# Moving the second half's weight loads behind the stores of x, tile 4's scores into slab 0, and the second pass's loads ahead in slab 8

## The chip, the cores and the metric

The kernel runs on one core of a Trainium2 chip. The metric is the device time of one execution in microseconds. Before the change it is 1320.05 us, the median of three runs (1319.97 to 1320.37). Names: TensorE (PE in the profile, PEld its weight loads), VectorE (DVE), ScalarE (ACT), GpSimd (POOL), SyncE (SP, which here issues every DMA).

## The reference, cut to what matters

Three layers follow each other on 4608 rows (8 batches of 576) of 512 columns:

```
scores = (q_c @ k_c^T) / 8            # chunks of 64 rows, 8 heads
attn = softmax(scores);  x = attn @ v # rows of 8 heads x 64 = 512 columns
xn = (x - mean) / sqrt(var + 1e-6) * g_ln
x2 = x + relu(xn @ w_ch1) @ w_ch2     # 512 -> 2048 -> 512
h = relu(x2 @ w_in)                   # 512 -> 1024
h = h * sigmoid(conv3(h, conv_w))     # three taps along the rows
out = h @ w_out                       # 1024 -> 512
```

The weights come as 64-bit numbers. Each matrix product is made of three matmuls on a high and a low part.

## The kernel before, in words

The rows are 36 tiles of 128, grouped in nine slabs of four tiles (512 rows). There are three passes.

**First pass.** For each tile `Attention` has one-letter steps: L loads q, k and v; S makes scores on TensorE; M takes their maxima on DVE; E is eight exponentials on ACT; R is a reciprocal on DVE; P transposes on TensorE; C copies on ACT; V multiplies by v on TensorE; X scales on DVE and stores x to DRAM (`xd`); B, x, T and e normalise the tile and put it, transposed, into the slab's block. `product` (L580) then multiplies the slab by w_ch1. It uses a scheme of seven products on quartered matrices, n = 1 to 7, for each of four column groups G. A slab so has 28 slots (`SLOTS`, L627). Its results are stored to `hd`.

w_ch1 is prepared from 64-bit numbers by `Block`, in sixteen pieces: W loads piece i, a is an ACT instruction (L134), t, m and n are DVE instructions (L140, L146, L152), g scales on ACT, s are sums on DVE, h and l make the high part (ACT) and the low part (DVE). W0 to W7 are the first half, which groups G = 0 and 1 need, W8 to W15 the second half, for G = 2 and 3. In the profile W is `w<-in_moe_w_ch_dram`.

The order is written out by hand. The string `START` (L18) lists the steps ahead of slab 0 and, behind the bar, those that are put into slab 0's slots one group after the other, separated by slashes. An engine works through its own instructions in this order, and so does SP with the DMAs. `session` (L634) places a tile's V, S of the next tile and so on into slots; L668 says at which slot the sessions of tiles 4 to 7 begin. Tiles use two buffers for q and k, three for v and two for x (tags `rq`, `rk`, `rv`, `x`), so that L4 waits for S2 and V1, L5 for S3 and V2, and X2 for the store of X0.

**Second pass.** `Down` (L670) loads a piece of `hd` (tag `hr`, three buffers of 512 KB), splits it into `hh` (ACT) and `hl` (DVE) and multiplies by w_ch2 (`w2`): 9 slabs of 16 steps. w_ch2 is prepared by `Piece`s: `cv_load` loads one, `cv_step` (L220) does one step of a pipeline of four (h, a, m, l) over the pieces. All this is begun in slab 8, behind the pool `dp` that takes the place of the attention's buffers from slot (G, s) = (0, 5). Four pieces lie in `dp` (`wd0` to `wd3`). The other twelve take the room of w_ch1's first half, from slot (2, 5) on. At a slab's end `finish` (L756) adds the residual and puts four `store`s into a list; each transposes a quarter on DVE into `x2T` and stores it to `x2d`. They are taken off one at a time in the next slab. Those of the last slab come together ahead of the third pass (L832).

**Third pass.** `Gate` and `outtile`: w_in, the taps, the gate, w_out. Gates write TensorE's banks 4 to 7 in turn, and `outtile` (L851) reads the high and low parts `Gh` and `Gl` of all eight gates.

Of the kernel before, what the change touches and what calls it, by code (L numbers as in the profile page):

```python
# [8 lines left out]
F32 = mybir.dt.float32  # L9
# [6 lines left out]


START = """  # L18
W0 W2 L0 W1 W3 L1 W4 W6 W5 L2 W7 L3 W8 W10 L4 W9 W11 W12 W14 W13 W15 L5
a0 t0 m0 n0 a2 t2 g0 m2 h0 n2 l0 g2 S0 M0 a1 t1 E0 m1 n1 t3 a3 P0 R0 g1  # L20
m3 C0 n3 S1 h1 g3 l1 V0 M1 h2 a4 l2 E1 X0 s0 t4 s2 a6 P1 s1 a5 t5 h4 s3
C1 m5 h3 l4 V1 m4 S2 l3 t6 h5 R1 m6 a7 t7 M2 X1 E2 n5 S3 B1 B0 g5 P2 R2
C2 M3 V2 y0 E3 n6 z0 y1 m7 n4 g6 P3 R3 n7 e0 X2 C3 z1 g7 l5 V3 e1 B2 h9
S4 X3 u1 h8 s4 g4 M4 h6 s6 h7 s5 E4 l6 s7 B3 h11 P4 y2 C4 l11 z2 y3 e2 l7
z3 v1 e3 l9 l8 u3 j0 u2 h10 v3 u5 v2 l10 v5 h12 j1 l12 u7 j2 h13 v7 u6 j3 l13
u4 v6 v4 R4
|
a8 t8 a10 t10 m8 n8
/ g8 a9 t9 m10 n10
/ g10 a11 a12 t11 t12 m9  # L30
/ a14 n9 t14 g9 m12
/ h14 n12 m11 g12 n11 a13
/ l14 t13 g11 m14 h15
/ n14 s8 g14 l15 a15
# [11 lines left out]
def attn_moe_moe2(  # L46
# [34 lines left out]
    NF1 = w_ch1.shape[1] // 128  # L81
# [174 lines left out]
    def add_w2(f, pool, tag):  # L256
        add(rows(w_ch2, f), w2, f, pool, tag)
# [261 lines left out]
    with tc.manual_schedule():  # L519
# [145 lines left out]
        for tv in range(4, NTILE):  # L665

            t = 28 * (tv // 4 - 1) + 7 * (tv % 4 - 1) + 1
            session({4: 1, 5: 8, 6: 12, 7: 16}.get(tv, t), tv)  # L668

        class Down:  # L670

# [21 lines left out]
            def down(self, f, hh, hl):  # L693
                for i in range(4):
                    s = slice(i * 128, (i + 1) * 128)
                    mm3(self.acc[i], hh[:, s], hl[:, s], w2[f][:, 0, :], w2[f][:, 1, :],
                        f == 0, f == NF1 - 1)

        F_ORDER = [f + 8 * i for f in range(8) for i in range(2)]
        dp = None  # L700
        for p in range(NS + 1):
            if p + 1 < NS:
                slabs[p + 1] = Slab(p + 1)
            for G in range(4):
                for s, (n, lag) in enumerate(SLOTS):
                    t = 28 * p + 7 * G + s
                    pp, GG = (p, G - lag) if G >= lag else (p - 1, 3)
                    if 0 <= pp < NS:
                        product(pp, GG, n)
                        nxt = slabs.get(pp + 1)  # L710
                        if GG == 3 and nxt:
                            if n == 1:
                                nxt.j(0)
                                nxt.j(1)
                            nxt.both(n)
                    for fn in events.pop(t, ()):
# [24 lines left out]
        su_p.release()
# [49 lines left out]
        downs = {0: down}  # L791
        xrs = {}
        for n, (p, f) in enumerate(todo):
            if n == 0:
                parts = down.split(f)
            hh, hl = parts

            if f < 8:
                ahead = p * 8 + f + 2
                if ahead < 8 * NS:  # L800
                    if ahead % 8 == 0:
                        downs[ahead // 8] = Down(ahead // 8)
# [12 lines left out]
            if (p, f) == (0, 15):  # L815
# [4 lines left out]
                for i in range(16):  # L820
                    pool, tag = wb_tags[i]
# [191 lines left out]
```

## Time and profile before

| what | value |
|---|---|
| median of three runs | 1320.05 us |
| the profiled execution, its own time | 1322.7 us |
| its span | 1320.8 us |
| TensorE busy | 1247.7 us (94%) |
| VectorE busy | 749.0 us (57%) |
| ScalarE busy | 615.6 us (47%) |
| mean granted TensorE clock | 0.968 |
| chain that ended last | TensorE 88%, DMA 5%, DVE 4%, ACT 2% |

The span runs from the first to the last instruction of the profiled execution; 1.9 us of its own time lie around it. The first pass begins its first product at 62.24 us, the second pass begins at 521.76 us and the third at 919.82 us of the span. In a timeline's row the bracket at the end is the idle time of the engine before this instruction and what released it.

### The profile page before, as it was taken

The page shows a single profiled execution, that of the slowest core. Times are in us where ns is not written, and L with a number is a line of the kernel's source. Part 1 is how long each engine was busy: PE and PEld are TensorE (multiplying, and loading weights), DVE is VectorE, ACT ScalarE, POOL GpSimd, SP SyncE. Part 2 cuts the span into 40 slices and gives each one's busy share as a digit, 9 for nine tenths or more (in the row PEclk, how much of TensorE's full clock was granted, in tenths as well). Part 3 has the DMA queues.
Part 4 walks back from the last instruction along what each step waited for, and adds up shares of the span by engine and source line. Part 5 has one row for each costly group of instructions (what it writes and reads, how often), then busy time and mean ns, then how long its engine had stood idle before and what let it go on. Part 6 is the DMA issues. An engine that isn't in the chain of part 4 may idle for free.

```text
span 1320.8 us, 23297 instructions
## 1 busy us (share of the span) xinstructions
PE 1247.7 (94%) x9096; PEld 1088.2 (82%) x9096; DVE 749.0 (57%) x1430; ACT 615.6 (47%) x1510; POOL 75.1 (6%) x172
## 2 busy tenths in 40 slices
PE   5468999999999996999999999999999999999998
PEld 4367999999999995787888888888888888888887
DVE  6597565565566455757743333433886555655550
ACT  6575565555565443433422223222675555555541
POOL 0000000000000000000000000000121111111000
PEclk6588999999999998999999999999999999999999
DMA  9523555545554348376543456443111011101001
GB/s 259 171 87 123 192 184 176 178 172 190 185 186 166 131 160 326 120 236 231 196 159 120 149 178 196 132 135 112 48 57 56 25 56 57 56 25 56 25 24 48
DMA packets 127021, 177.70 MB, mean 135 GB/s; under 512 B 12736, under 2 KB 72128, under 8 KB 126912
## 3 DMA queue, kind: packets, MB, share of 16 engines
q1 hardware_dynamic: 126912, 176.22, 40.2%
q8 instruction: 71, 1.16, 0.4%
q14 instruction: 38, 0.31, 0.1%
HBM read 110.13 MB, written 66.06 MB: 133 GB/s over the span
## 4 chain that ended last, share of the span: by engine, by line
PE 88%; DMA 5%; DVE 4%; ACT 2%; SPq 0%; issue 0%; POOL 0%; DVEq 0%; ACTq 0%; POOLq 0%
PE banks L114 28%; PE banks L115 27%; PE banks L116 27%; DMA w<-in_moe_w_ch_dram 2%; PE banks L381 2%; PE banks L463 1%; DMA rq<-in_q_dram 1%; PE banks L421 1%; DVE w L157 1%; DMA hr<-hd 1%; DMA xd<-x 1%; DMA wd<-in_moe_w_ch_dram 0%; DVE xr L160 0%; ACT pp L407 0%; ACT w L336 0%
## 5 line engine op out<-in xcount | busy, mean ns | idle before, releaser
L114 PE MATMUL banks<-xc,w 128*128 128x256 f32 x1008 | 289.9, 288 | 6.6 <-ACT u L606 5.8
L115 PE MATMUL banks<-xc,w 128*128 128x256 f32 x1008 | 282.6, 280 | 0.6 <-DVE xc L157 0.6
L116 PE MATMUL banks<-xc,w 128*128 128x256 f32 x1008 | 282.1, 280 | 0.0
L686 ACT ACTIVATE hh<-hr 128x512 fp32r<-128x512 f32 x144 | 90.9, 632 | 279.0 <-PE banks L116 269.5
L687 DVE SCALAR_TENSOR_TENSOR hl<-hr,hh 128x512 fp32r<-128x512 f32 x144 | 99.2, 690 | 204.9 <-ACT hh L686 204.9
L114 PEld LDWEIGHTS banks<-xc,w 128*128 128x128 f32 x1008 | 192.5, 191 | 10.0 <-ACT u L606 6.5
L115 PEld LDWEIGHTS banks<-xc,w 128*128 128x128 f32 x1008 | 192.9, 191 | 0.8 <-DVE xc L157 0.8
L116 PEld LDWEIGHTS banks<-xc,w 128*128 128x128 f32 x1008 | 192.7, 191 | 0.0
L114 PE MATMUL banks<-w,hl 128*128 128x512 f32 x432 | 168.5, 390 | 0.0
L115 PE MATMUL banks<-w,hh 128*128 128x512 f32 x432 | 168.1, 389 | 0.0
L116 PE MATMUL banks<-w,hh 128*128 128x512 f32 x432 | 168.1, 389 | 0.0
L897 DVE SCALAR_TENSOR_TENSOR cv<-hb,cw_sb,cv 128x510 f32<-128x510 f32 (+31 forms) x256 | 117.3, 513 | 0.6
L115 PE MATMUL banks<-xb,w 128*128 128x512 f32 x288 | 113.0, 392 | 0.0
L114 PE MATMUL banks<-xb,w 128*128 128x512 f32 x288 | 112.9, 392 | 0.0
L116 PE MATMUL banks<-xb,w 128*128 128x512 f32 x288 | 112.8, 392 | 0.0
L160 DVE TENSOR_TENSOR u<-banks,u 128x512 f32<-128x512 f32 x108 | 73.6, 689 | 60.0 <-ACT u L606 32.8
L114 PEld LDWEIGHTS banks<-w,hl 128*128 128x128 f32 x432 | 81.1, 188 | 18.3 <-DVE hl L687 1.4
L116 PEld LDWEIGHTS banks<-w,hh 128*128 128x128 f32 x432 | 81.1, 188 | 17.0
L115 PEld LDWEIGHTS banks<-w,hh 128*128 128x128 f32 x432 | 81.1, 188 | 16.5
L606 ACT COPY u<-banks 128x512 f32<-128x512 f32 x108 | 64.0, 593 | 59.9 <-PE banks L116 56.8
L407 ACT ACTIVATE pp<-banks,mx 128x64 f32<-128x64 f32 x288 | 87.7, 333 | 3.3 <-DVE mx L398 2.8
L115 PE MATMUL banks<-w,Gh 128*128 128x512 f32 x216 | 84.3, 390 | 0.0
(106 smaller groups left out, 2095.0 us busy)
## 6 DMA issues: line engine op xcount, KB each, us to landing
hd<-u SPq DMA_DIRECT2D x144, 256.0 KB, 3.0
hr<-hd SPq DMA_DIRECT2D x72, 512.0 KB, 4.1
w<-in_moe_w_ch_dram SPq DMA_DIRECT2D x28, 512.0 KB, 7.6
rv<-in_v_dram SPq DMA_DIRECT2D x36, 256.0 KB, 4.0
xd<-x SPq DMA_DIRECT2D x36, 256.0 KB, 2.0
xr<-xd SPq DMA_DIRECT2D x36, 256.0 KB, 5.1
x2d<-x2T SPq DMA_DIRECT2D x36, 256.0 KB, 2.1
x2r<-x2d SPq DMA_DIRECT2D x36, 256.0 KB, 4.1
```

The lines of the kernel that those rows point to most:

```text
L114: nc.tensor.matmul(ps, ll, rh, start=first, stop=False, **kw)
L115: nc.tensor.matmul(ps, lh, rl, start=False, stop=False, **kw)
L116: nc.tensor.matmul(ps, lh, rh, start=False, stop=last, **kw)
L157: nc.vector.tensor_tensor(out=out, in0=a, in1=b, op=ALU.subtract)
L160: nc.vector.tensor_tensor(out=out, in0=a, in1=b, op=ALU.add)
L381: nc.tensor.matmul(ps[half(c), e, j, :], lt[half(e), j, c, :], rt[half(e), j, c, :], start=True, stop=True,)
L407: nc.scalar.activation(out=pp[:, j, e, :], in_=self.both[T][:, e, j, :], func=AF.Exp, scale=SCALE, bias=mx[:, e, j:j + 1], accum_out=sm[:, ...
L421: nc.tensor.transpose(tp[:, j * 128:(j + 1) * 128], pp[:, j].rearrange("p e k -> p (e k)"), ident)
L606: nc.scalar.copy(flat(t), bank[to])
L686: nc.scalar.activation(out=self.hh, in_=t, func=AF.Relu)
L687: nc.vector.scalar_tensor_tensor(out=self.hl, in0=t, scalar=0.0, in1=self.hh.bitcast(F32), op0=ALU.max, op1=ALU.subtract,)
L897: nc.vector.scalar_tensor_tensor(out=cv[:, a:e], in0=hb[:, a + tap:e + tap], scalar=cw_sb[:, tap, f:f + 1], in1=cv[:, a:e], op0=ALU.mult, ...
```

## The change

`START` loses W8 to W15, L4 and L5 from its first lines; they stand behind the stores that belong to X1, X2 and X3. W7 goes ahead of L2. S4, M4 and E4 go from the part ahead of slab 0 into its slot 0, R4 and P4 into slot 2, C4 into slot 3. The other steps ahead of slab 0 are put into another order. The sessions of tiles 4 to 7 begin one slot later, that of tile 4 four slots later.

In slab 8, the second pass's first three loads of `hd` are issued at slot (0, 5), ahead of the loads of w_ch2. Five pieces of w_ch2 instead of four lie in `dp`. The steps of `cv_step` are left out of slots (2, 6) to (3, 6) but for (3, 1), (3, 3) and (3, 5). The first split is made at slot (3, 4). Later loads of `hd` are issued at odd steps for three pieces ahead, instead of at even steps for two. `x2T` has one buffer instead of two.

```diff
 START = """
-W0 W2 L0 W1 W3 L1 W4 W6 W5 L2 W7 L3 W8 W10 L4 W9 W11 W12 W14 W13 W15 L5
-a0 t0 m0 n0 a2 t2 g0 m2 h0 n2 l0 g2 S0 M0 a1 t1 E0 m1 n1 t3 a3 P0 R0 g1
...
-S4 X3 u1 h8 s4 g4 M4 h6 s6 h7 s5 E4 l6 s7 B3 h11 P4 y2 C4 l11 z2 y3 e2 l7
...
+W0 W2 L0 W1 W3 L1 W4 W6 W5 W7 L2 L3 a0 t0 m0 n0 a2 t2 g0 m2 h0 n2 l0 g2
...
+E1 X0 s0 t6 s2 a6 s1 P1 a5 t5 s3 h4 R1 h3 m6 C1 l2 m5 V1 B0 S2 X1 W8 W10
...
+R3 g7 y0 l5 C3 z0 y1 h9 V3 X2 W9 W11 L4 W12 e0 l9 g4 z1 X3 W14 W13 W15 L5 h8
...
 |
-a8 t8 a10 t10 m8 n8
+S4 M4 E4 a8 t8 a10 t10 m8 n8
 / g8 a9 t9 m10 n10
-/ g10 a11 a12 t11 t12 m9
-/ a14 n9 t14 g9 m12
+/ g10 a11 a12 t11 t12 m9 R4 P4
+/ C4 a14 n9 t14 g9 m12
...
-            session({4: 1, 5: 8, 6: 12, 7: 16}.get(tv, t), tv)
+            session({4: 5, 5: 9, 6: 13, 7: 17}.get(tv, t), tv)
...
+        EARLY = 5
...
-                            for i, f in enumerate(F_ORDER[:4]):
+                            down = Down(0)
+                            for f in range(3):
+                                down.load(f)
+                            for i, f in enumerate(F_ORDER[:EARLY]):
                                 add_w2(f, lambda: dp, f"wd{i}")
                             cv_load(2)
...
-                            cv_load(12)
-                        elif (G, s) > (0, 5) and s % 2 == 0:
+                            cv_load(NF1)
+                        elif (0, 5) < (G, s) < (2, 5) and s % 2 == 0 or (G, s) in ((3, 1), (3, 3), (3, 5)):
                             cv_step()
-                        if (G, s) == (3, 2):
-                            down = Down(0)
-                            for f in range(2):
-                                down.load(f)
+                        if (G, s) == (3, 4):
+                            parts = down.split(0)
...
-                    x2T = dp.tile([128, 512], F32, tag="x2T", bufs=2, name="x2T")
+                    x2T = dp.tile([128, 512], F32, tag="x2T", bufs=1, name="x2T")
...
-            if n == 0:
-                parts = down.split(f)
...
-            if f < 8:
-                ahead = p * 8 + f + 2
+            if f >= 8:
+                ahead = p * 8 + f % 8 + 3
```

On SP's queue, ahead of slab 0, before the change (the last of the second half's weights, then L5, then the first stores of x, `xd_99` being that of tile 0):

```order
L125 DMA w_281<-in_moe_w_ch_dram 128x1024
L125 DMA w_283<-in_moe_w_ch_dram 128x1024
L125 DMA w_285<-in_moe_w_ch_dram 128x1024
L366 DMA rq<-in_q_dram 64x2x256 x2
L366 DMA rk<-in_k_dram 64x2x256 x2
L375 DMA rv<-in_v_dram 128x512
L439 DMA xd_99<-x 128x512
L439 DMA xd_100<-x 128x512
L439 DMA xd_101<-x 128x512
```

The same place now, from L3 on:

```order
L365 DMA rq<-in_q_dram 64x2x256 x2
L365 DMA rk<-in_k_dram 64x2x256 x2
L374 DMA rv<-in_v_dram 128x512
L438 DMA xd_99<-x 128x512
L438 DMA xd_100<-x 128x512
L124 DMA w_449<-in_moe_w_ch_dram 128x1024
L124 DMA w_451<-in_moe_w_ch_dram 128x1024
L438 DMA xd_101<-x 128x512
L124 DMA w_579<-in_moe_w_ch_dram 128x1024
L124 DMA w_581<-in_moe_w_ch_dram 128x1024
```

The first stores have gone from behind L5 to right behind L3, with W8 and W10 (`w_449`, `w_451`) next.

On ACT, at slab 0's slot 0, before (`u_749` is the copy of its first product, L134 the steps a8 and a10, L311 g8):

```order
L606 COPY u_749<-banks 128x512
L134 ACTIVATE w_751<-w_263 128x512
L134 ACTIVATE w_754<-w_265 128x512
L311 ACTIVATE w_751<-w_751,g_sb 128x512
L134 ACTIVATE w_751<-w_275 128x512
```

and now:

```order
L605 COPY u_712<-banks 128x512
L406 ACTIVATE pp,sm<-banks,mx 128x64 x8
L133 ACTIVATE w_743<-w_449 128x512
L133 ACTIVATE w_746<-w_451 128x512
L310 ACTIVATE w_743<-w_743,g_sb 128x512
```

E4's eight exponentials now stand ahead of a8.

On SP's queue in slab 8, around slot (0, 5), before (`hd_0_167` is a store of the slab's own results, `wd` a piece of w_ch2):

```order
L601 DMA hd_0_167<-u_6583 128x512
L125 DMA wd_6664<-in_moe_w_ch_dram 128x1024
L125 DMA wd_6666<-in_moe_w_ch_dram 128x1024
L601 DMA hd_0_167<-u_6680 128x512
L125 DMA wd_6686<-in_moe_w_ch_dram 128x1024
```

and now:

```order
L600 DMA hd_0_167<-u_6583 128x512
L679 DMA hr<-hd_0_135 128x4x256 x2
L679 DMA hr<-hd_1_136 128x4x256
L124 DMA wd_6670<-in_moe_w_ch_dram 128x1024
L124 DMA wd_6672<-in_moe_w_ch_dram 128x1024
L600 DMA hd_0_167<-u_6686 128x512
```

Three loads of 512 KB for the second pass stand ahead of the first weight piece.

## Rows read from the trace of the kernel before

**Rows 1.** The page's 40 slices of the span, TensorE's busy share in tenths.

```profile
PE   5468999999999996999999999999999999999998
```

**Rows 2.** Stretches: busy us (instructions) per engine, granted clock, DMA share, GB/s.

```profile
0.00:30.00 30.00, 15.97 (x192) 12.19 (x192) 18.83 (x38) 17.91 (x54) 0.85 (x8) 0.67 0.97 253
...
60.00:90.00 30.00, 20.57 (x239) 19.07 (x238) 29.25 (x58) 21.86 (x50) 0.63 (x2) 0.80 0.18 54
```

**Rows 3.** The chain that ended last: start us, us, what.

```profile
44.31 6.91 DMA xd<-x
...
96.80 1.20 ACT pp L407 x8
...
510.01 10.32 DMA hr<-hd
```

**Rows 4.** DVE's timeline ahead of and in slab 0.

```profile
29.50 0.43 DVE L140 TENSOR_SCALAR w<-w 128x512 int32<-128x512 uint32 x1 [1.97 <-DMA w<-in_moe_w_ch_dram]
...
51.32 0.69 DVE L435 TENSOR_TENSOR x<-banks,sm 128x512 f32<-128x512 f32 x1 [12.72 <-DMA xd<-x]
...
71.45 0.71 DVE L140 TENSOR_SCALAR w<-w 128x512 int32<-128x512 uint32 x2
...
73.41 0.68 DVE L397 TENSOR_REDUCE mx<-banks 128x8 f32<-128x512 f32 x1
...
109.29 0.69 DVE L445 BATCH_NORM_STATS2 bs<-x 128x6 f32<-128x512 f32 x1
...
110.30 0.68 DVE L157 TENSOR_TENSOR w<-w,w 128x512 fp32r<-128x512 f32 x1
...
113.09 0.69 DVE L157 TENSOR_TENSOR w<-s,w 128x512 fp32r<-128x512 f32 x1 [0.68 <-ACT w L336]
```

**Rows 5.** ACT's timeline in slab 0: a8 and a10, then a15.

```profile
70.44 1.23 ACT L134 ACTIVATE w<-w 128x512 f32<-128x512 f32 x2
...
87.53 0.68 ACT L134 ACTIVATE w<-w 128x512 f32<-128x512 f32 x1
```

**Rows 6.** TensorE's timeline in slab 8 and into the second pass.

```profile
480.56 0.39 PE L114 MATMUL banks<-xc,w 128*128 128x256 f32 x1 [1.95 <-ACT u L606]
...
503.17 0.39 PE L114 MATMUL banks<-xc,w 128*128 128x256 f32 x1 [1.65 <-ACT u L606]
...
509.57 0.38 PE L114 MATMUL banks<-xc,w 128*128 128x256 f32 x1 [0.68 <-ACT u L606]
...
521.76 0.29 PEld L114 LDWEIGHTS banks<-wd,hl 128*128 128x128 f32 x1 [9.38 <-DVE hl L687]
```

**Rows 7.** ACT's timeline in slab 8: the first two pieces of w_ch2.

```profile
479.34 0.69 ACT L134 ACTIVATE cy<-wd 128x512 f32<-128x512 f32 x1 [4.18 <-DMA wd<-in_moe_w_ch_dram]
...
480.99 0.67 ACT L134 ACTIVATE cy<-wd 128x512 f32<-128x512 f32 x1 [0.48 <-DMA wd<-in_moe_w_ch_dram]
```

**Rows 8.** Stretches of slab 8 and the second pass's start.

```profile
478.40:487.00 8.60, 6.65 (x44) 6.46 (x44) 5.21 (x9) 5.07 (x9) 0.00 (x0) 0.80 0.66 249
487.00:498.00 11.00, 11.00 (x100) 11.00 (x99) 7.45 (x13) 3.98 (x7) 0.00 (x0) 1.00 0.35 126
...
521.70:527.00 5.30, 5.24 (x15) 4.18 (x16) 2.94 (x6) 1.27 (x3) 0.00 (x0) 0.62 1.00 346
527.00:537.00 10.00, 10.00 (x46) 8.26 (x45) 9.49 (x17) 6.68 (x12) 0.00 (x0) 1.00 0.20 64
```

**Rows 9.** DVE's timeline at the third pass's start, and the low part of gate 7.

```profile
920.63 1.29 DVE L762 STREAM_TRANSPOSE x2T<-xr 128x512 f32<-128x512 f32 x2
923.47 1.37 DVE L762 STREAM_TRANSPOSE x2T<-xr 128x512 f32<-128x512 f32 x2 [1.55 <-DMA x2d<-x2T]
...
956.00 0.69 DVE L931 TENSOR_TENSOR Gl<-gt,Gh 128x511 fp32r<-128x511 f32 x1
```

**Rows 10.** ACT's timeline at the third pass's start.

```profile
927.07 0.72 ACT L886 ACTIVATE cv<-hb,cw_sb 128x511 f32<-128x511 f32 x1 [0.85 <-DMA x2d<-x2T]
```

**Rows 11.** TensorE's timeline: the first `outtile` reads gate 7's low part.

```profile
957.90 0.39 PE L114 MATMUL banks<-wx,Gl 128*128 128x512 f32 x1
```

More of the change, by code (lines that the diff above doesn't have):

```diff
@@ L18 @@
 START = """
-W0 W2 L0 W1 W3 L1 W4 W6 W5 L2 W7 L3 W8 W10 L4 W9 W11 W12 W14 W13 W15 L5
-a0 t0 m0 n0 a2 t2 g0 m2 h0 n2 l0 g2 S0 M0 a1 t1 E0 m1 n1 t3 a3 P0 R0 g1
-m3 C0 n3 S1 h1 g3 l1 V0 M1 h2 a4 l2 E1 X0 s0 t4 s2 a6 P1 s1 a5 t5 h4 s3
-C1 m5 h3 l4 V1 m4 S2 l3 t6 h5 R1 m6 a7 t7 M2 X1 E2 n5 S3 B1 B0 g5 P2 R2
-C2 M3 V2 y0 E3 n6 z0 y1 m7 n4 g6 P3 R3 n7 e0 X2 C3 z1 g7 l5 V3 e1 B2 h9
-S4 X3 u1 h8 s4 g4 M4 h6 s6 h7 s5 E4 l6 s7 B3 h11 P4 y2 C4 l11 z2 y3 e2 l7
-z3 v1 e3 l9 l8 u3 j0 u2 h10 v3 u5 v2 l10 v5 h12 j1 l12 u7 j2 h13 v7 u6 j3 l13
-u4 v6 v4 R4
+W0 W2 L0 W1 W3 L1 W4 W6 W5 W7 L2 L3 a0 t0 m0 n0 a2 t2 g0 m2 h0 n2 l0 g2
+S0 M0 a1 t1 E0 m1 n1 t3 a3 P0 R0 g1 m3 C0 n3 S1 h1 g3 l1 V0 M1 h2 a4 t4
+E1 X0 s0 t6 s2 a6 s1 P1 a5 t5 s3 h4 R1 h3 m6 C1 l2 m5 V1 B0 S2 X1 W8 W10
+a7 t7 M2 m7 E2 n5 l3 S3 n6 m4 g5 P2 M3 g6 C2 n4 E3 V2 l4 n7 B1 h5 R2 P3
+R3 g7 y0 l5 C3 z0 y1 h9 V3 X2 W9 W11 L4 W12 e0 l9 g4 z1 X3 W14 W13 W15 L5 h8
+h7 B2 e1 B3 h6 u1 l7 v1 y3 l8 z3 s4 e3 y2 s6 z2 s5 e2 l6 h11 j0 u2 j1 u3
+s7 u5 v3 u7 h10 l11 j2 l10 u6 v2 h12 v6 j3 l12 u4 v5 h13 v4 l13 v7
 |
-a8 t8 a10 t10 m8 n8
+S4 M4 E4 a8 t8 a10 t10 m8 n8
 / g8 a9 t9 m10 n10
-/ g10 a11 a12 t11 t12 m9
-/ a14 n9 t14 g9 m12
+/ g10 a11 a12 t11 t12 m9 R4 P4
+/ C4 a14 n9 t14 g9 m12
 / h14 n12 m11 g12 n11 a13
@@ L729, in attn_moe_moe2 @@
                             tags = [f"w0{kk}{i}" for kk in range(2) for i in range(7)]
-                            for f, tag in zip(F_ORDER[4:], tags):
+                            for f, tag in zip(F_ORDER[EARLY:], tags):
                                 add_w2(f, lambda: wa_p, tag)
-                            cv_load(12)
-                        elif (G, s) > (0, 5) and s % 2 == 0:
+                            cv_load(NF1)
+                        elif (0, 5) < (G, s) < (2, 5) and s % 2 == 0 or (G, s) in ((3, 1), (3, 3), (3, 5)):
                             cv_step()
-                        if (G, s) == (3, 2):
-                            down = Down(0)
-                            for f in range(2):
-                                down.load(f)
+                        if (G, s) == (3, 4):
+                            parts = down.split(0)
         su_p.release()
```

## The prediction, made before the changed kernel was run

> **What bounds the kernel now.** I read the page's slices first. TensorE is busy all along except in two places: the first slices, ahead of and in slab 0, and the slices around 480 to 520 us [rows 1]. What the change saves must come out of these two, so I went on with stretches, then with the chain of waits, then with each engine's timeline there.
>
> Ahead of slab 0 and in its first half the engine that sets the pace is DVE, which prepares w_ch1: in 60 to 90 us it is busy for 29.25 of 30 us, TensorE for 20.57 [rows 2]. The one long hole in DVE's time is the instruction X2, which waits 12.72 us, to 51.32, for the store of X0 [rows 4]. The chain says why: that store is issued only at 44.31 and takes 6.91 us to land [rows 3], for in SP's order it stands behind all sixteen weight pieces and L5. TensorE runs on without holes when the list of weight steps ends, with DVE's last low part at 113.09 [rows 4].
>
> Around 480 to 520 us slab 8 goes over into the second pass. TensorE's timeline has four holes there: 1.95, 1.65 and 0.68 us for ACT's copies out of its banks, and 9.38 us for the first `hl` [rows 6]. The copies are late because ACT stands in front of a weight piece that hasn't landed (4.18 us for the first) [rows 7], the `hl` because its load of `hd`, issued at 510.01 behind twelve weight loads, lands after 10.32 us [rows 3].
>
> The sum below is made against the profiled execution (1322.7 us, span 1320.8). It lies 2.65 us above the median of 1320.05; I take the same saving off the median.
>
> **Term 1, ahead of and in slab 0.** The store of X0 now stands right behind L3 and is long landed when X2 comes: **-12.7 us** on DVE. W7 ahead of L2 takes away DVE's wait of 1.97 us for W7 [rows 4], and L2's transfers, S2 and M2 come later by about one weight load (1.65 us, from the two landings seen at 479.34 and 480.99 [rows 7]); I let the two cancel. M4, some 0.7 us (the maximum at 73.41 [rows 4]), only moves along DVE's queue. E4 does cost something: it was hidden in ACT's idle time during the 12.72 us, and now stands ahead of a8 in slot 0, with DVE's m8 behind a8. M4 must first get through on DVE, then ACT needs 2 x 1.20 us for eight exponentials [rows 3] and about 0.6 for a8 [rows 5], of which DVE fills 0.71 with t8 and t10 [rows 4]: 2.4 + 0.6 - 0.7 = **+2.3 us**. The session of tile 6 begins at slot 13 instead of 12, so that its statistics (109.29 to 110.30 [rows 4]) come behind the list's last weight step: **-1.0 us**. Sum: -12.7 + 2.3 - 1.0 = **-11.4 us**. The weight loads themselves I cost at nothing: W8 follows X1's store, some 30 us ahead of a8, and the first 30 us move 253 GB/s [rows 2], so that eight loads of 0.52 MB take some 17 us; if this cover goes, each late load stops ACT and DVE in turn (a rival below). Bounds: 7 us saved (ACT behind the exponentials and copies also stops DVE later in slab 0, about twice the 2.3) to 15 us (DVE's small waits for ACT near 113 us go too).
>
> **Term 2, slab 8.** Removed: with `hd` loaded at slot (0, 5) and split at (3, 4), the hole of 9.38 us goes. With no weight step between (2, 5) and (3, 1), ACT's stop at 502 us goes, and with it 1.65 + 0.68 us. The half clock behind the 9.38 us goes too: in 521.7 to 527 us the granted clock is 0.62 (that is, partly 1.2 GHz) and 15 matmuls take 5.24 us, where 46 take 10.00 at full clock [rows 8]: 15 x (0.349 - 0.217) = 2.0 us. Removed in all: 9.4 + 1.65 + 0.7 + 2.0 = 13.7 us.
>
> Added: at (0, 5) three loads of 512 KB now stand ahead of the first weight piece, and the step at (0, 6) still makes ACT wait for that piece, with the copy behind it that frees TensorE's bank. No row shows these loads in this place. If the transfers overlapped fully, the piece would land as now: 0. If each took the 4.18 us that ACT waited for one [rows 7], end to end, 12.5 us. The nearest row is the spacing of two weight loads issued together, 480.99 - 479.34 = 1.65 us [rows 7], and the load of `hd` behind twelve others that took 10.32 us [rows 3] shows that later loads do wait their turn: 3 x 1.65 = **+5.0 us**. The hole of 1.95 us becomes 6.9. After it there is a stretch at half clock already now (clock 0.80; 44 matmuls in 6.65 us where 100 take 11.00 [rows 8]: 44 x (0.151 - 0.110) = 1.8 us); after a longer hole I take the 2.0 us seen behind the 9.38: +0.2. Term 2: -13.7 + 5.0 + 0.2 = **-8.5 us**, bounds -13.5 and -1.
>
> The Trainium skill, page "DMA: Bandwidth & Descriptors", section "Queues, rings and completion order", says that a DMA engine consumes the descriptors of one ring in order; by that rule the weight piece does wait for the three loads, which speaks against this order of issue, and the row of 10.32 us agrees. From the ceiling of 435 GB/s in the same page's "Specifications" the three loads would take 3.6 us, an estimate, and the result would be 1.4 us lower.
>
> Costed at nothing: the fifth piece in `dp` (its steps fill the eight slots up to (2, 4)); the later loads of `hd` (three steps ahead, queued behind nothing that waits); the weight steps moved out of slab 8 (the last piece is ready five steps ahead of its use, and DVE's work in each step of the second pass stays the same).
>
> **Term 3, the third pass's start.** With one `x2T`, the last slab's four transposes run one after the other with their stores. The row at 923.47 shows the interval: it waited for the store of the one at 920.63, 2.84 us [rows 9]. The fourth so begins at 920.63 + 3 x 2.84 = 929.15 instead of about 924.1: DVE 5.0 us late. What comes next on ACT had already waited 0.85 us for such a store [rows 10], and the chain of gates has 957.90 - 956.69 = 1.2 us to spare when TensorE needs gate 7's low part [rows 9, 11]; the banks of the gates leave about as much. Up to there ACT and DVE wait for each other and catch nothing up: 5.0 - 0.85 - 1.2 = **+3.0 us**. Bounds: 0 (four banks of lead hide it) and 5.0. Inside the second pass the stores come 5 us apart, more than 2.84, and cost nothing.
>
> **Sum**: -11.4 - 8.5 + 3.0 = -16.9 us; 1320.05 - 16.9 = 1303.15, rounded to **1303 us** (a profiled execution would stand near 1306).
>
> **The rivals.**
> A. *The loads of `hd` don't delay the weight piece*: SP issues them in time that the transfers don't need, and ACT waits its 4.18 us as now. For it: the DMA engines are not full at this place (share 0.66 in 478.4 to 487 [rows 8]). Against it: the 10.32 us. Then 5.2 us less: 1298 us.
> B. *The third pass hides its late start.* For it: TensorE does not wait once there now. Against it: 1.2 us to spare only. Then 1300 us.
> C. *Slab 0 keeps more*: with E4 and a tighter row of sessions ACT becomes the bound between slots 0 and 13. For it: E4 comes in addition to ACT's 21.86 us of 30 [rows 2]. Against it: 8 us of idle time are left there. Term 1 at -7: 1307.5 us.
> D. *The change doesn't take the wait away*: X2 or X3 waits as long for something else, such as V2. Against it: L2 and L3 still stand ahead of every store. Then term 1 is near 0: 1314.5 us.
> E. *Slower: the second half's weights come too late for slab 0.* Six of them, L4 and L5 are now issued only behind the stores of X2 and X3, at about 39 us (51.32 - 12.72 [rows 4]). If queued loads landed 10.32 us apart, as long as that one load took [rows 3], the sixth would land at 39 + 62 = 101; from its a step (a15, 87.53 [rows 5]) to the list's end DVE needs 113.8 - 87.5 = 26 us, so the list ends at 127 instead of 113.8: +13.5, less the 5.5 of terms 2 and 3, so 1328 us. It decides from (113.8 + 5.5 - 26 - 39) / 6 = 9 us a load. Against it: 253 GB/s, or 2 us a load [rows 2].
>
> **How the numbers follow.** Forecast 0.50, A 0.15, B 0.10, C 0.17, D 0.05, E 0.03. The range of **1296 to 1311** takes in A and B, alone or with term 1 at its upper bound in part (1303 - 5.2 - 3 = 1295), and on the other side C, or the loads of `hd` end to end (+7.5: 1310.5). What is left out is D, E and the joint ends. About 0.2% (2.6 us) is what a measurement of this kernel can tell from no change. Every case but E lies over 0.2% below 1320.05: faster 0.95; same 0.02, for several upper bounds together; slower 0.03.
>
> **What would show it.** In the changed profile: no wait of DVE for `xd<-x`; TensorE's unbroken work from about 104 us; DVE idle some 2 us behind M4 in slot 0; in slab 8 ACT waiting some 9 us for `wd` and TensorE with one hole of about 7 us, then half clock, but no hole ahead of the second pass; four single transposes 2.84 us apart at the end, and short waits of TensorE in the third pass's first ten gates. A hole of 2 us in slab 8 would prove term 2 wrong on `hd`; DVE or ACT waiting for `w<-in_moe_w_ch_dram` in slab 0 would prove rival E right.

## The result, and the profile after

The changed kernel takes **1309.25 us** (median of 4 runs, 1308.23 to 1310.14), the kernel before beside it 1320.21 (4 runs, 1319.97 to 1322.01): a ratio of 0.9914 with an interval of 0.9897 to 0.9931, so 9.1 to 13.6 us less, 11.3 by the ratio in the middle. The forecast was 1303, 16.9 us less. The profiled execution took 1309.48 us (span 1307.5).

Every stage can be dated by one row of TensorE's timeline. I use five marks throughout, and the end of the span (session 8 is that of tile 8, session 35 that of the last tile):

| mark (us from the span's start) | before | after | difference | gained in the stage |
|---|---|---|---|---|
| session 8's product with v | 127.91 | 118.00 | -9.91 | -9.91 |
| session 35's product with v | 447.19 | 437.21 | -9.98 | -0.07 |
| second pass, first matmul | 521.76 | 505.70 | -16.06 | -6.08 |
| third pass, first gate | 919.82 | 903.25 | -16.57 | -0.51 |
| third pass, first output tile | 953.12 | 939.81 | -13.31 | +3.26 |
| end of the span | 1320.8 | 1307.5 | -13.3 | 0 |

So the two profiles differ by 13.3 us where the ratio of the medians gives 11.3; the profiled execution of before lies high among its runs (1322.7 against medians of 1318.1 to 1320.6 in all comparisons).

The page's slices of the changed kernel, TensorE's row (for [rows 1]) and the granted clock:

```profile
PE   5559999999999989999999999999999999999998
...
PEclk6689999999999989999999999999999999999999
```

Slab 0 is full one slice earlier; the dent at 495 to 528 us (the sixteenth slice) is gone, and a weaker one stands a slice earlier, at 458 to 490 us, in slab 8. DVE's timeline ahead of and in slab 0 (start, duration, engine, line, operation, operands, count; in brackets the idle time ahead and its releaser), to be laid beside [rows 4]:

```profile
36.77 0.68 DVE L434 TENSOR_TENSOR x<-banks,sm 128x512 f32<-128x512 f32 x1
...
55.30 0.68 DVE L396 TENSOR_REDUCE mx<-banks 128x8 f32<-128x512 f32 x1
...
59.34 0.69 DVE L145 SCALAR_TENSOR_TENSOR w<-w,w 128x512 int32<-128x512 int32 x1 [2.49 <-ACT w L133]
...
83.19 0.69 DVE L396 TENSOR_REDUCE mx<-banks 128x8 f32<-128x512 f32 x1 [3.54 <-PE banks L380]
...
99.81 0.69 DVE L396 TENSOR_REDUCE mx<-banks 128x8 f32<-128x512 f32 x1 [1.62 <-PE banks L380]
...
104.01 0.69 DVE L156 TENSOR_TENSOR w<-s,w 128x512 fp32r<-128x512 f32 x1 [0.69 <-ACT w L335]
```

X2 no longer waits for its store: it runs at 36.77 instead of 51.32. But the list's last low part comes at 104.01, only 9.1 us earlier: DVE has three new holes, 2.49 us for a8 behind M4 as forecast, and 3.54 and 1.62 us for TensorE's scores, which the forecast did not have. TensorE's timeline shows who is late there:

```profile
81.07 1.13 PE L380 MATMUL banks<-rv,pt 64*64 64x64 f32 x32 [3.04 <-ACT pt L426]
...
97.69 1.13 PE L380 MATMUL banks<-rv,pt 64*64 64x64 f32 x32 [5.74 <-ACT pt L426]
...
118.00 0.69 PE L380 MATMUL banks<-rv,pt 64*64 64x64 f32 x32
```

The products of tiles 5 and 6 wait for ACT's copy `pt` of the same tile, which stands in the same slot.

Slab 8, first SP's issues, then ACT, TensorE, and the windows (PE, PEld, DVE, ACT and POOL busy, granted clock, DMA share, GB/s), for [rows 6 to 8]:

```profile
464.36 1.94 SPq L679 DMA_DIRECT2D hr<-hd  x3
466.35 1.19 SPq L124 DMA_DIRECT2D wd<-in_moe_w_ch_dram  x2
```

```profile
473.88 0.69 ACT L133 ACTIVATE cy<-wd 128x512 f32<-128x512 f32 x1 [8.71 <-DMA wd<-in_moe_w_ch_dram]
```

```profile
475.10 0.58 PE L113 MATMUL banks<-xc,w 128*128 128x256 f32 x1 [6.46 <-ACT u L605]
...
502.12 0.38 PE L113 MATMUL banks<-xc,w 128*128 128x256 f32 x1 [0.68 <-ACT u L605]
504.21 0.39 PE L113 MATMUL banks<-xc,w 128*128 128x256 f32 x1 [0.45 <-DVE u L159]
505.70 0.39 PE L113 MATMUL banks<-wd,hl 128*128 128x512 f32 x1
```

```profile
475.00:480.00 5.00, 4.90 (x29) 4.91 (x30) 2.99 (x6) 4.08 (x8) 0.00 (x0) 0.65 0.97 328
480.00:490.00 10.00, 10.00 (x91) 10.00 (x90) 9.66 (x17) 4.44 (x8) 0.00 (x0) 1.00 0.31 112
```

ACT's wait for the first weight piece has grown from 4.18 to 8.71 us, and TensorE's hole from 1.95 to 6.46; behind it the clock is at 0.65, 29 matmuls taking 4.90 us where 91 take 10.00 at full clock (some 1.7 us). The hole of 9.38 us ahead of the second pass is gone.

Inside the second pass the changed order of issue makes a new wait. The first row below is the kernel before, where ACT takes up conv_w (the taps, `cw_raw`) without a wait. The others are the changed kernel, on ACT, on TensorE and on SP's queue:

```profile
566.26 0.21 ACT L134 ACTIVATE cw_sb<-cw_raw 128x24 f32<-128x24 f32 x1
...
552.71 0.22 ACT L133 ACTIVATE cw_sb<-cw_raw 128x24 f32<-128x24 f32 x1 [3.89 <-DMA cw_raw<-in_moe_conv_w_dram]
...
554.24 0.50 PE L113 MATMUL banks<-wd,hl 128*128 128x512 f32 x1 [0.65 <-DVE hl L686]
...
531.19 16.18 SPq L679 DMA_DIRECT2D hr<-hd  x4
547.43 3.23 SPq L196 DMA_DIRECT2D cw_raw<-in_moe_conv_w_dram  x3
```

The loads of `hd`, now three pieces ahead, wait on SP's queue until DVE's `hl` of an earlier piece frees a buffer, and conv_w's load stands behind the fourth of these four: it is issued 41.7 us after the pass's first matmul, against 37.8 before (559.52 - 521.76). The split `hh` of a later piece stands behind it on ACT.

The third pass's start on DVE, and TensorE's first waits for it, for [rows 9 to 11]:

```profile
904.06 0.70 DVE L763 STREAM_TRANSPOSE x2T<-xr 128x512 f32<-128x512 f32 x1
906.88 0.71 DVE L763 STREAM_TRANSPOSE x2T<-xr 128x512 f32<-128x512 f32 x1 [2.12 <-DMA x2d<-x2T]
...
912.52 0.71 DVE L763 STREAM_TRANSPOSE x2T<-xr 128x512 f32<-128x512 f32 x1 [2.11 <-DMA x2d<-x2T]
```

```profile
923.22 0.50 PE L113 MATMUL banks<-xb,w 128*128 128x512 f32 x1 [0.21 <-ACT hb L881]
927.49 0.50 PE L113 MATMUL banks<-xb,w 128*128 128x512 f32 x1 [1.20 <-ACT hb L881]
```

The four transposes now stand singly, 2.82 us apart; TensorE now waits in the first gates, and the stage is 3.26 us longer.

### The profile page after: what moved, and what is told of

Read it like the earlier page. It is cut to its first block, busy times and chain, and to the rows that moved or that the text cites. A ratio compares the mean times of both kernels' runs of the same rounds, so it can differ in the third digit from the quotient of the medians.

```text
span 1307.5 us, 23314 instructions
## 1 busy us (share of the span) xinstructions
PE 1249.2 (96%) x9096; PEld 1087.0 (83%) x9096; DVE 748.9 (57%) x1430; ACT 614.8 (47%) x1510; POOL 76.2 (6%) x172
## 4 chain that ended last, share of the span: by engine, by line
PE 85%; DVE 6%; ACT 4%; DMA 3%; issue 1%; SPq 1%; POOL 0%; DVEq 0%; ACTq 0%; POOLq 0%
PE banks L113 27%; PE banks L114 26%; PE banks L115 26%; PE banks L380 3%; PE banks L462 1%; PE banks L420 1%; DMA w<-in_moe_w_ch_dram 1%; DVE w L156 1%; ACT pp L406 1%; DMA wd<-in_moe_w_ch_dram 1%; DVE w L151 0%; DMA x2d<-x2T 0%; ACT w L335 0%; DVE xr L159 0%; DVE w L145 0%
## 5 line engine op out<-in xcount | busy, mean ns | idle before, releaser
L113 PE MATMUL banks<-w,hl 128*128 128x512 f32 x396 | 154.7, 391 | 0.0
L114 PE MATMUL banks<-w,hh 128*128 128x512 f32 x396 | 154.1, 389 | 0.0
L115 PE MATMUL banks<-w,hh 128*128 128x512 f32 x396 | 154.1, 389 | 0.0
L113 PEld LDWEIGHTS banks<-w,hl 128*128 128x128 f32 x396 | 74.3, 188 | 17.4 <-DVE hl L686 2.1
L115 PEld LDWEIGHTS banks<-w,hh 128*128 128x128 f32 x396 | 74.3, 188 | 15.6
L114 PEld LDWEIGHTS banks<-w,hh 128*128 128x128 f32 x396 | 74.3, 188 | 15.2
L883 POOL COPY hal<-hb 128x2 f32<-128x2 f32 x64 | 41.8, 652 | 736.6 <-ACT hb L881 736.6
```

Source lines behind the costliest of these rows:

```text
L113: nc.tensor.matmul(ps, ll, rh, start=first, stop=False, **kw)
L114: nc.tensor.matmul(ps, lh, rl, start=False, stop=False, **kw)
L115: nc.tensor.matmul(ps, lh, rh, start=False, stop=last, **kw)
L883: nc.gpsimd.tensor_copy(out=hal[:, f, :], in_=hb[:, 512:514])
```

## The experiments

Open were: whether the gains of the two halves are separate; what has eaten the rest of X2's 12.7 us; whether the loads of `hd` cause the hole in slab 8; and what paces the third pass's start. The marks of all runs (us; "slab 8" is session 35 to the second pass, "start 3" the third pass's first gate to its first output tile), and the ratios to the kernel before with their intervals:

| run | session 8 | slab 8 | start 3 | span | median us | ratio |
|---|---|---|---|---|---|---|
| before | 127.91 | 74.57 | 33.30 | 1320.8 | 1320.21 | |
| changed | 118.00 | 68.49 | 36.56 | 1307.5 | 1309.25 | 0.9914 [0.9897, 0.9931] |
| e1 | 119.04 | 71.84 | 33.30 | 1309.2 | 1310.42 | 0.9930 [0.9915, 0.9946] |
| e2 | 127.59 | 67.50 | 36.53 | 1314.7 | 1317.44 | 0.9985 [0.9973, 0.9996] |
| e3 | 117.81 | 68.50 | 36.56 | 1306.3 | 1308.16 | 0.9912 [0.9894, 0.9930] |
| e4 | 118.47 | 68.00 | 34.29 | 1305.0 | 1306.39 | 0.9898 [0.9882, 0.9914] |
| e5 | 119.46 | 61.56 | 36.54 | 1300.3 | 1302.65 | 0.9881 [0.9865, 0.9898] |
| e6 | 117.34 | 67.06 | 36.56 | 1303.8 | 1305.89 | 0.9906 [0.9888, 0.9924] |
| e7 | 117.40 | 69.15 | 36.57 | 1307.1 | 1306.59 | 0.9916 [0.9900, 0.9933] |
| e8 | 121.26 | 72.93 | 33.30 | 1311.4 | 1314.00 | 0.9968 [0.9956, 0.9980] |
| e9 | 114.51 | 61.30 | 34.29 | 1295.7 | 1295.59 | 0.9814 [0.9801, 0.9828] |
| e10 | 116.43 | 60.49 | 34.28 | 1293.7 | 1294.92 | 0.9810 [0.9796, 0.9824] |
| e11 | 115.75 | 60.59 | 33.30 | 1292.1 | 1292.86 | 0.9807 [0.9791, 0.9824] |
| e12 | 113.24 | 72.81 | 33.30 | 1302.0 | 1305.67 | 0.9903 [0.9886, 0.9920] |

### e1 and e2: the two halves apart

e1 is the kernel before with the new list and this line; e2 is the changed kernel with both undone.

```diff
-            session({4: 1, 5: 8, 6: 12, 7: 16}.get(tv, t), tv)
+            session({4: 5, 5: 9, 6: 13, 7: 17}.get(tv, t), tv)
```

> The kernel before with the new list of weight steps and the new session slots alone; slab 8 and the second pass as before. Theory (the terms stand apart, and term 1 is worth what the changed kernel's profile showed at session 8): session 8's first product begins at about 118.1 us instead of 127.98, TensorE's hole of some 9.4 us ahead of the second pass and the one of 1.95 us in slab 8 are still there, the third pass starts as before; 9.9 us less than before, so 1310.3 us, a ratio of 0.9925. Rival (part of the gain depends on the second half's changes, or is given back at slab 8, where the loads meet other traffic): less than 7 us, ratio above 0.9947.

> The changed kernel with the list of weight steps and session slots of before; slab 8, second pass and the single x2T buffer as changed. Theory: session 8 at 128.0 as before, from there the milestones of the changed kernel: second pass 6.1 us earlier, 6.6 at the third pass's first gate, 3.3 given back in its first gates; 3.3 us less than before, so 1316.9 us, ratio 0.9975. Prediction's terms 2 and 3: -5.5 us, 1314.7, ratio 0.9958. Rival (the loads of hd at (0, 5) are delayed by what slab 0 does, so that term 2 is different without it): a hole in slab 8 other than 6.5 us by over 1 us.

e1 came out at 0.9930 (0.9925 expected), e2 at 0.9985 (0.9975), its hole in slab 8 at 6.23 us. The product of the two ratios is 0.9915, the changed kernel's own 0.9914: the halves add, and most of the gain is the first one. e1 tells one more thing, in TensorE's timeline at the start of the second pass, which this kernel has as before:

```profile
510.13 0.79 PE L113 MATMUL banks<-wd,hl 128*128 128x512 f32 x1 [6.50 <-DVE hl L686]
```

The hole that the forecast took at 9.38 us (9.19 in the matmul's own row) is 6.50 here, and slab 8 takes 71.84 us instead of 74.57. In e8 and e12, which also leave the second half alone, it takes 72.93 and 72.81.

### e8 and e12: the wait for the store of X0 by itself

Both are built on the kernel before, with nothing moved but loads. e8 (each piece of the list with its neighbours):

```diff
-L3 W8 W10 L4 W9 W11 W12 W14 W13 W15 L5 a0
+L3 a0
-X1 E2
+X1 W8 W10 E2
-X2 C3
+X2 W9 W11 L4 W12 C3
-X3 u1
+X3 W14 W13 W15 L5 u1
```

> The kernel before with one thing changed: W8 to W15, L4 and L5 are issued behind the stores of X1, X2 and X3, at the places in the list that the changed kernel has for them; the rest of the list, the sessions and the second half as before. Theory (X2's 12.72 us were the wait for the store of X0, queued behind all the loads): the wait goes, and as E4, the session slots and the order of the steps stay as they were, session 8 begins 12 us or more earlier than 127.9, more than the changed kernel's 9.9: at 114 to 117. Rival (the wait only passes on, since DVE then meets ACT's and TensorE's chain of the four tiles; what the changed kernel gains needs the rest of its reordering): DVE idles elsewhere ahead of slab 0 by over 4 us and session 8 begins at 119 or later.

The theory fell, the rival held: session 8 at 121.26. DVE's timeline shows the wait in a new place:

```profile
48.47 0.69 DVE L397 TENSOR_REDUCE mx<-banks 128x8 f32<-128x512 f32 x1 [7.56 <-PE banks L381]
```

That is M4; tile 4's scores had waited 7.24 us for `rk`, the k that L4 loads, now issued at 40.63, behind the store of X2. So e12 moves L4 alone:

```diff
-X1 W8 W10 E2
+X1 L4 W8 W10 E2
-X2 W9 W11 L4 W12 C3
+X2 W9 W11 W12 C3
```

> The run with only the loads behind the stores (built on the kernel before), with one more edit: L4 right behind the store of X1 instead of behind that of X2. Theory (in that run tile 4's scores waited 7.24 us for their k, since L4 was issued at 39 us behind the store of X2, and DVE's next maximum waited 7.56 us behind them; this is why the changed kernel has to take tile 4's scores into slab 0): the k lands by about 37 us, DVE's hole falls from 7.56 us to under 2, and session 8 begins at 115 to 116 instead of 121.3, as early as or earlier than in the changed kernel, with S4, M4 and E4 where they were. Rival (ACT's and TensorE's chain of tile 4 takes that time anyway): session 8 at 119 or later.

Session 8 begins at 113.24, a little better than expected and 4.8 us earlier than in the changed kernel. DVE's row for the same M4, and TensorE's for session 8:

```profile
40.41 0.69 DVE L397 TENSOR_REDUCE mx<-banks 128x8 f32<-128x512 f32 x1
```

```profile
113.24 0.69 PE L381 MATMUL banks<-rv,pt 64*64 64x64 f32 x32
```

With nothing but loads moved, session 8 begins 14.5 us earlier in this execution (127.75, the mean of before and e2, less 113.24), and the whole of e12 has a ratio of 0.9903, as much as the changed kernel with all its parts. Moving tile 4's scores into slab 0 is one cure for a late L4; issuing L4 earlier is a cheaper one.

### e6, e7 and e10: what is lost inside slab 0

The timed ratios of e6 and e7 can't be told from the changed kernel's, so these runs rest on their traces. The start of slab 0 wanders by up to 1.9 us between executions of the same code; I therefore read the time from TensorE's first product after its wait for `xc` to session 8. It is 64.37 us in the changed kernel (53.63 to 118.00) and 64.19 to 64.37 in e1, e3, e4 and e5, which share its first half. The measure has its own scatter: e9 and e11, which have one and the same slab 0, differ by 1.05 us in it (59.74 and 60.79), so single runs can't be told apart by much less than that. e6:

```diff
-            session({4: 5, 5: 9, 6: 13, 7: 17}.get(tv, t), tv)
+            session({4: 4, 5: 9, 6: 13, 7: 17}.get(tv, t), tv)
```

> The changed kernel with the session of tile 4 one slot earlier (4 instead of 5), so that tile 5's transposes, copy and product stand in two slots and no longer in one. Theory (three sessions exactly four slots apart put P, C and V of a tile into one slot, so that TensorE waits for ACT in the middle of it and DVE for TensorE behind it): TensorE's wait of 3.04 us for ACT's pt at slot 9 and DVE's hole of 3.54 us behind it go, the 5.74 us at slot 13 stays; session 8 begins 2 to 3.5 us earlier than 118.0. Rival C of the prediction (ACT's own work is the bound between slots 0 and 13): the idle time turns up elsewhere on DVE or TensorE and session 8 moves by less than 1 us.

It takes 62.20 us, 2.1 less than the mean of the five, as the theory has it. By the mark that was on record the rival's sign came, not the theory's: session 8 is only 0.7 us earlier, because this execution's first product came 1.5 us later. The measure used here is not the one on record. TensorE's timeline at slots 9 and 13:

```profile
80.05 0.69 PE L380 MATMUL banks<-rv,pt 64*64 64x64 f32 x32 [1.37 <-ACT pt L426]
...
96.88 1.13 PE L380 MATMUL banks<-rv,pt 64*64 64x64 f32 x32 [5.29 <-ACT pt L426]
```

The 3.04 us are down to 1.37, and DVE's 3.54 us are gone (a hole of 1.96 us for tile 5's scores, a few slots earlier, is new); the wait at slot 13 stays. e7:

```diff
-S4 M4 E4 a8 t8 a10 t10 m8 n8
+a8 t8 a10 t10 S4 M4 E4 m8 n8
```

> The changed kernel with a8 t8 a10 t10 ahead of S4 M4 E4 in slot 0. Theory (E4's eight exponentials stand ahead of a8 on ACT, and DVE's next low bits behind a8): DVE's idle 2.49 us at 59.34 goes or falls under 0.5, and session 8 begins up to 2.5 us earlier than 118.0. Rival (E4 then comes later and with it P4, C4 and V4, so that the time is lost again behind them): session 8 within 0.7 us of 118.0.

61.97 us, 2.3 less; DVE's hole of 2.49 us behind M4 is gone, and nothing comes back for it on DVE. Here too the mark itself moved by 0.6 us only, the rival's sign, with a first product 1.8 us later. e10 (below) also takes away the wait at slot 13, with sessions at 3, 8, 13 and 17: 61.21 us, against 59.74 and 60.79 in e9 and e11, which keep 5.28 us there. So taking away TensorE's longest wait in slab 0 gains nothing that can be seen. In e10 two new waits stand behind it, for DVE's weight step `w` and for ACT's copy `u`, 5.28 us together:

```profile
97.08 0.38 PE L113 MATMUL banks<-xc,w 128*128 128x256 f32 x1 [2.39 <-DVE w L156]
...
102.64 0.39 PE L113 MATMUL banks<-xc,w 128*128 128x256 f32 x1 [2.89 <-ACT u L605]
```

e10 moves the sessions of tiles 4 and 5 and C4 as well, so it is no clean test of that one wait. A wait of TensorE counted where DVE stood still behind it (3.54 us at slot 9); at slot 13 DVE waits 1.62 us only. That DVE is the bound there is the reading that fits these rows; no run took DVE's own work away.

### e3 and e5: the loads of `hd` and the weight pieces

e3 issues two pieces first:

```diff
-down = Down(0)
-for f in range(3):
-    down.load(f)
 for i, f in enumerate(F_ORDER[:EARLY]):
     add_w2(f, lambda: dp, f"wd{i}")
 cv_load(2)
+down = Down(0)
+for f in range(3):
+    down.load(f)
```

> The changed kernel with the first two weight pieces of the second pass issued ahead of the three loads of hd at slot (0, 5). Theory (the three loads delay the piece, 4.5 us in the profile, and TensorE stops for it): ACT's wait for the first piece falls from 8.71 us to about 4.2, TensorE's hole from 6.46 to about 2.0, half clock behind it stays; 4.5 us less than the changed kernel, so 1304.7 us, ratio to before 0.988. The loads of hd then land some 4 us later, which nothing waits for until slot (3, 4). Rival (the piece is late by itself, the loads share the engines without order): ACT waits 7 us or more, and the time stays within 1.5 us of 1309.2.

Half of it came true: ACT gets the first piece after 3.38 us, and the time does not change. ACT's timeline and TensorE's:

```profile
467.33 0.69 ACT L133 ACTIVATE cy<-wd 128x512 f32<-128x512 f32 x1 [3.38 <-DMA wd<-in_moe_w_ch_dram]
...
469.27 0.69 ACT L133 ACTIVATE cy<-wd 128x512 f32<-128x512 f32 x1 [0.78 <-DMA wd<-in_moe_w_ch_dram]
...
477.01 0.68 ACT L133 ACTIVATE cy<-wd 128x512 f32<-128x512 f32 x1 [6.06 <-DMA wd<-in_moe_w_ch_dram]
```

```profile
468.55 0.38 PE L113 MATMUL banks<-xc,w 128*128 128x256 f32 x1 [1.14 <-ACT u L605]
...
478.22 0.58 PE L113 MATMUL banks<-xc,w 128*128 128x256 f32 x1 [5.32 <-ACT u L605]
```

The third piece, issued at 467.15 behind the loads of `hd` (464.10), is late in place of the first: 1.14 + 5.32 us of hole against 6.46. e5 lets no piece stand behind the loads:

```diff
-down = Down(0)
-for f in range(3):
-    down.load(f)
...
+if (G, s) == (1, 4):
+    down = Down(0)
+    for f in range(3):
+        down.load(f)
```

> The changed kernel with the three loads of hd issued at slot (1, 4), behind the fifth and last weight piece of slab 8, instead of at (0, 5). Theory (three runs of one queue land in the order of issue: whatever piece stands behind the loads of hd is late by them, the first in the changed kernel with 6.46 us, the third with 5.32 us when two pieces went ahead): no piece stands behind them now, so ACT waits some 3.4 us for the first piece and less than 1 us for the others, TensorE has one hole of 1 to 2 us, and session 8's start to the second pass's first product takes some 5.5 us less than the 387.7 of the changed kernel: 382 us; time 1303.5 us, ratio 0.988. The first hl stays ready in time. Rival (slab 8's pieces are late because each step asks for a piece one step after its issue, loads of hd or not): holes of 4 us or more in sum remain, time above 1306.

ACT's first piece and TensorE's only hole of over 1 us in the slab:

```profile
468.70 0.68 ACT L133 ACTIVATE cy<-wd 128x512 f32<-128x512 f32 x1 [4.06 <-DMA wd<-in_moe_w_ch_dram]
```

```profile
469.90 0.39 PE L113 MATMUL banks<-xc,w 128*128 128x256 f32 x1 [1.81 <-ACT u L605]
```

Slab 8 takes 61.56 us instead of 68.49. That is more than the 4.65 us of hole, because the half clock behind it does not come either (granted clock 1.00 from 459.5 to 509.5; in the changed kernel it cost 1.7); the 0.45 us for DVE are gone too. The Trainium skill, page "DMA: Bandwidth & Descriptors", section "Queues, rings and completion order", says that a DMA engine takes the descriptors of one ring in order; the three orders of issue agree.

### e4, e9, e10 and e11: the third pass's start, and all together

e4 gives the last slab's four stores buffers of their own:

```diff
-x2T = dp.tile([128, 512], F32, tag="x2T", bufs=1, name="x2T")
+if T < 4 * NS - 4:
+    x2T = dp.tile([128, 512], F32, tag="x2T", bufs=1, name="x2T")
+else:
+    x2T = dp.tile([128, 2, 512], F32, tag=f"wd{i}", bufs=1, name="x2T")[:, 0]
```

> The changed kernel, but the last slab's four transposes write four buffers of their own (the second pass's first four weight tiles, read for the last time before). Theory (term 3: the chain of four transposes and stores, 2.8 us apart, is what the third pass starts late by): transposes end to end, no wait for x2d's stores, and the time from the third pass's first gate to its first output tile falls by 3.3 us to at most 33.3 us; 3.3 us less than the changed kernel, so 1306 us, ratio 0.9892. Rival (the gates' start is paced by ACT's and DVE's own work, or by the loads of conv_w): the gap falls by less than 1 us, time within 1 us of 1309.2.

The transposes run end to end, but only 2.27 of the 3.3 us come back. e9 takes `x2T` and the three `hr` buffers instead, with the edits of e5, e6 and e7 and this one, by which slab 8's steps begin a slot later:

```diff
-elif (0, 5) < (G, s) < (2, 5) and s % 2 == 0 or ...
+elif (0, 6) < (G, s) < (2, 5) and s % 2 == 0 or ...
```

> The changed kernel with five edits together: loads of hd at slot (1, 4); the steps of slab 8's weight pieces one slot later, from (1, 0) on; the last slab's stores of x2d from x2T and the three hr buffers; tile 4's session at slot 4; a8 t8 a10 t10 ahead of S4 M4 E4. Theory (the losses found so far are separate and add up): session 8 at about 114 us (118.5 on the mean of five runs, less 2.1 and 2.3); from there to the second pass about 377 us (378.9, less the hole of 1.8 in slab 8); from the third pass's first gate to its first output tile 33.3 us as in the kernel before, with the transposes end to end and no wait of ACT for a store; span about 1290 us, time 1292, ratio 0.980. Rival (the two edits of slab 0 free the same idle time and don't add; the buffers of hr too lie under something that the third pass writes at once): session 8 at 116 or later, or over 34 us to the first output tile; time 1295 or more.

Session 8 is where it was expected (114.51), the time 3.6 us above the 1292, so that the second half of the rival held. Start 3 is 34.29 us again, and ACT's timeline of e9 shows why, as e4's does with the same length:

```profile
898.45 0.60 ACT L886 ACTIVATE hb<-banks 128x512 f32<-128x512 f32 x1 [10.31 <-DMA x2d<-x2T]
```

The first gate's tile `hb` waits for the last store, 10.31 us where it waits 7.61 us for TensorE in the changed kernel. The reading is that both sets of buffers lie where the third pass puts that tile; no run shows the addresses. e10 is e9 with these places in the list and the sessions:

```diff
-/ g10 a11 a12 t11 t12 m9 R4 P4
-/ C4 a14 n9 t14 g9 m12
+/ g10 a11 a12 t11 t12 m9 R4 P4 C4
+/ a14 n9 t14 g9 m12
-            session({4: 4, 5: 9, 6: 13, 7: 17}.get(tv, t), tv)
+            session({4: 3, 5: 8, 6: 13, 7: 17}.get(tv, t), tv)
```

> As the run of the five edits together, but with the sessions of tiles 4 to 7 at slots 3, 8, 13 and 17 and C4 a slot earlier, so that only tile 7's copy and product share a slot. Theory (the 5.74 us of TensorE at slot 13 is tile 6's transposes, copy and product in one slot): that wait goes too, and session 8 begins another 1 to 4 us earlier than with slots 4, 9, 13 and 17. Rival (DVE's list of weight steps now sets the end by its own work; nothing is left to gain): session 8 within 1 us of the other.

The theory fell: session 8 is no earlier, but 1.9 us later than in e9 and 0.7 us later than in e11, whose slab 0 is e9's. That there is nothing to gain is what the rival said, though against e9 its bound of 1 us is not kept. e11 is e9 with the stores in the buffers of the weight conversion, idle by then:

```diff
-    x2T = dp.tile([128, 4, 256], F32, tag="hr", bufs=3, name="x2T")
+    x2T = dp.tile([128, 512], F32, tag="cy", bufs=4, name="x2T")
```

> The run of the five edits together (sessions 4, 9, 13, 17), with the last slab's four stores of x2d taken from the four buffers cy of the weight conversion instead of x2T and hr. Theory (with two sets of buffers tried, ACT's first gate waited 10.31 us for the last store, because its tile hb lay over one of them; cy lies under a tile that the third pass writes only later): ACT's wait for x2d is gone, the time from the third pass's first gate to its first output tile is 33.3 us as in the kernel before, where 34.29 was measured with the other sets; 1 us less, so 1294 us or a little under, ratio 0.980. Rival (the third pass's start is paced by the casts of x2r and the gates' own chain, whatever the stores wait for): 34.3 us again.

```profile
893.95 0.60 ACT L885 ACTIVATE hb<-banks 128x512 f32<-128x512 f32 x1 [7.61 <-PE banks L115]
```

ACT waits for TensorE alone, start 3 is 33.30 us, and e11 is the fastest run here: 1292.86 us, ratio 0.9807, which can't be told from e9's and e10's by their intervals. The edit that shifts the steps of slab 8 was worth little: 60.5 to 61.3 us instead of e5's 61.56, though the hole of 1.81 us is gone: a hole of 0.96 to 1.35 us for a copy of ACT comes nearer the slab's end in its place. e12's loads together with e11's second half were not run; by the marks of session 8 (113.24 and 115.75) that would be some 2.5 us less again, an estimate from one execution of each.

## Why the forecast was right in kind and too large in size

The range held and the order of the terms was right. By the means of all runs that share a stage, the changed kernel's 11.3 us come out of four sums: session 8 at 118.56 (changed, e1, e3, e4, e5) instead of 127.75, **-9.2**; slab 8 in 68.1 us (changed, e2, e3, e4, e6, e7) instead of 73.0 (before, e1, e8, e12), **-4.9**; the second pass **-0.6**; the third pass's start **+3.3**. Sum -11.4.

**Term 1 (-11.4, measured -9.2).** The mechanism held: the 12.7 us were the wait for a store queued behind loads, and E4 ahead of a8 cost the 2.3 us that e7 gives back. The step that failed is the sessions: the forecast gave the new slots a gain of 1.0 us and no price. With tiles 5 to 7 exactly four slots apart, a tile's transposes, copy and product fall into one slot; e6 measures 2.1 us for the first of the three. The forecast's bound "ACT behind the exponentials and copies also stops DVE later in slab 0" named it, with rival C, at 7 us saved; it was put on ACT's load, where it is the order within a slot, as e6 shows by moving one number. The gain of 1.0 us itself came: the statistics stand at 104.62 us, behind the list's last low part at 104.01. With the missing +2.1 the sum is -9.3, and -9.2 was measured; that they agree so closely is partly luck, since e6's 2.1 us is good to about 1 us. And L2 with the scores "cancel" was an argument over small waits; the large one beside it, L4 behind the stores, was not seen as the reason for moving tile 4's scores at all.

**Term 2 (-8.5, measured -4.9 in slab 8 and -0.6 in the second pass).** The added wait was right: 5.0 forecast, 4.53 measured on ACT, and a hole of 6.46 for 6.9; rival A (the loads delay nothing) is refuted by e3 and e5. By stage the forecast has -6.5 in slab 8 and -2.0, the half clock, in the second pass; 1.6 and 1.4 us of them are missing.

In slab 8 what was mis-sized is the hole for the first `hl`. It came from one execution; by the matmuls' rows it is 9.19 us there and 6.50, 8.91 and 7.03 in e1, e8 and e12. All four holes of that place make 13.47 us before, and 10.87, 12.65 and 11.73 in these three: 1.7 us less on the mean. The 0.68 us that were to go with ACT's stop stayed, with 0.45 us for DVE behind it: 1.1 us. Against these 2.8 us, the added wait was 0.5 us shorter and the half clock behind it 0.3 us cheaper than forecast.

In the second pass the half clock did go: by its 60th matmul the seven kernels with the changed second half are 2.1 us ahead of the four without (13.62 us from the pass's first matmul instead of 15.73). But they give 1.5 us back. Some 0.8 us of it go between the 192nd and the 216th matmul, where ACT waits for conv_w: 3.5 to 4.1 us in all seven (and in e9 to e11), not at all in before, e1, e8 and e12. The step that failed is that the later loads of `hd` were costed at nothing, as "queued behind nothing that waits": what counts is what is queued behind them. The waits show this; no run moved conv_w's load by itself, and where the other 0.7 us go was not found.

**Term 3 (+3.0, measured +3.26).** The mechanism held, and the size within 0.3 us: 2.82 us between transposes, TensorE waiting in the first ten gates. The two reductions in its sum (0.85 and 1.2) were not measured one by one. Rival B is refuted by the same marks in all runs with one `x2T`, 36.53 to 36.57.

**The rivals D and E.** X2 did not wait for anything else, and DVE and ACT have no wait for `w<-in_moe_w_ch_dram` in slab 0.

**The profiled execution.** The forecast noted that it lay 2.65 us above the median and took the sum off the median; but what is longer than usual in that execution alone cannot also be saved from the median. Two candidates show: the four holes from slab 8 to the second pass (13.47 us against a mean of 11.75), which the change removes in part, and the stretch from session 8 to session 35 (319.28 us, where the shortest are 317.4), which it does not touch. How the 2.65 us divide between them was not settled.

## What to carry to other kernels

A load that nobody needs yet is not free if something urgent is issued behind it on the same queue: put it behind the last urgent one, not merely behind the first. Before moving compute to make room for a late load, try to move the load. When a wait is removed, read the size of it from more than one execution where there are several, and look at what the next instruction on the same engine waits for; twice here (e8, e4) the wait only changed its name. And when loads are issued further ahead, look at what stands behind them on the queue.

## What the runs showed that was not expected

- TensorE's stretch from session 8 to session 35 has the same instructions in all fourteen kernels and no wait of any length, and yet takes 317.4, 318.3 or 319.3 us. In the long ones one or two slabs run with 12.06 us from session to session instead of 11.72. What does it was not found.
- When the longest single wait of TensorE in slab 0 (5.74 us in the changed kernel, 5.28 in e9) went, nothing was gained (e10), while cutting one of 3.04 us to 1.37 came with 2.1 us.
- A buffer that is free in its own pool can still hold up the next stage: with the last stores from two sets of buffers (e4, e9) ACT's first `hb` waited 10.31 us, for the store; from the third (e11) 7.61 us, for TensorE, as it does in the changed kernel. What lay at their addresses next is the reading that fits.
